# A fused attention and gated-FFN kernel on one core: another order of all five queues, another choice of engines, and one transposition done another way

## The chip, the core and the metric

The kernel runs on one core of one Trainium2 chip. The core has five instruction queues that run side by side and meet only through semaphores: TensorE (PE in the profile; its weight loads are shown apart as PEld), VectorE (DVE), ScalarE (ACT), GpSimd (POOL) and SyncE (SP). POOL and SP mostly issue DMAs here. The metric is the device time of one execution in microseconds. Three runs of the kernel before took 198.94 to 199.34 us, median 199.04.

## What is computed

Attention over pooled keys and values, then a feed-forward layer with a gated convolution over the sequence:

```python
k_p = k.reshape(B, H, Sp, 8, D).mean(axis=3)          # B=8, H=8, S=576, D=64, Sp=72
v_p = v.reshape(B, H, Sp, 8, D).mean(axis=3)
scores = np.matmul(q, k_p.transpose(0, 1, 3, 2)) / 8
attn = softmax(scores)
x = (attn @ v_p) as [B, S, 512]
h = np.maximum(x @ w_in, 0.0)                          # [B, S, 1024]
conv = sum over k in 0..2 of conv_w[k] * h shifted by k - 1 along S
out = (h * sigmoid(conv)) @ w_out                      # [B, S, 512], float32
```

Inputs are float32; the kernel computes in bfloat16 with float32 accumulation.

## The kernel before, in words

The batch elements b = 0..7 each go through the same stages; several are in flight at once.

- **Loads.** POOL issues DMAs that cast float32 to bfloat16: `ldk{b}.0` (512 rows of k, 512 KB as stored) and `ldk{b}.t` (64 rows), `ldv{b}.0` (512 KB; batch 0 has two of 256 KB, `ldv0.0` and `ldv0.1`) and four tails of 16 KB `ldv{b}.t0` to `.t3`, `ldq{b}` (576 KB), and the weights `ldwi0` (256 KB), `ldwi1`, `ldwo0`, `ldwo1`. POOL also builds the identity and, in five steps `mask0` to `mask4` (L371, L375), the mask that the v blocks need. k, v and q have two buffers each, so a load of batch b + 2 waits until batch b is done with its buffer.
- **Pooling.** DVE adds the eight rows of each pool (`kp1`, `kp2`, `ksum` for k, L414, L418, L443; `vp1`, `vp2`, `va`, `vb` for v). PE turns k (`kT`, L459), ACT or DVE copies it out (`kz`, L465).
- **q.** It has to be turned, too, and there are three ways: straight from the loaded layout in pairs of heads (`qTP`, L545, three groups of 16 matmuls with 64 columns of weights), from a regrouped copy (`qg` on DVE, L257, then `qT`, three groups of 8 matmuls with 128 columns), or by a transposing DMA from the regrouped copy (`qD` on SP, L566). `PARAMS["alt"]` says which batch uses which.
- **Attention.** `sc` (scores, five tiles per batch), `exp` on ACT (L610), `av` (attention times v with the row sums, L628 and L632, five tiles), `rc` and `nm` on DVE (reciprocal and normalising into `xx`, L641 and L645; four `xx` buffers), and the turn of x into `xT`: by matmul (`xt`, L659, and a copy `xte`) for batches 0 to 2, by a transposing DMA on SP (`xD`, L668) for 3 to 7.
- **Feed-forward.** `mm1.b.f` (eight matmuls of 288 columns, L700, for each of 8 blocks f of 128 hidden columns; it needs all five tiles of `xT`), `relu` on ACT (L706), then the convolution. In most blocks it is three steps outside PE: two scalings `cp0` and `cp2` (ACT L722 or DVE L724), two additions `ca0` and `ca2` (DVE L729, L734); in ten blocks PE does it (L753). `tanh` on ACT (L741, L758), `tg1` and `g` on DVE (L785, L791) make the gated product gT for two blocks at once.
- **Output.** `mm2.pair.t.c` (eight matmuls of 512 columns, L813, one tile of 128 rows; two batch elements form a pair with nine tiles), `oe` copies the tile out (ACT L836), `st` on SP stores one or two tiles (L840). For the last pair the tiles 4 to 8 are done in two pieces, so that only two of the eight products wait for the last gate.
- **Fillers.** Before some PE steps stand products of a zero tile (`fill`, L227), which compute nothing and keep PE occupied. The kernel has 238 of them.

No order follows from loops at run time. `Planner.add` numbers each step in the order in which the program text makes it, and `PARAMS["order"]` is a list of these numbers; each engine gets its steps in the order in which they stand in that list. `123@A1` also says which PSUM buffer the step takes (three of two banks, A0 to A2, and two of one bank, B0 and B1), and `23A1/93@B0` puts 23 fillers ahead of step 93. `PARAMS["act"]` names the steps that run on ACT where DVE could do them as well. The durations in the `add` calls have no effect on what runs.

```python
if slot:
    self.held[o.take] = (slot[0], int(slot[1]))
e = next(iter(o.eng)) if len(o.eng) == 1 else "ACT" if o.name in self.on_act else "DVE"
out.append((e, o, warm))
```

Of the kernel before, what the change touches and what calls it, by code (L numbers as in the profile page):

```python
# [13 lines left out]

PARAMS = {
    "order": (
# [40 lines left out]
    ),  # L57
    "act": (
# [8 lines left out]
    ),  # L67
    "alt": {"w": 1, "q1": 1, "c0.5": 2, "c0.7": 2, "q2": 1, "c1.1": 1, "c1.3": 2, "q3": 1, "x3.0": 1, "x3.1": 1, "x3.2": 1, "x3.3": 1, "x3.4": 1, "c2.1": 1, "c2.5": 1, "q4": 1, "x4.0": 1, "x4.1": 1, "x4.2": 1, "x4.3": 1, "x4.4": 1, "c3.5": 1, "q5": 1, "x5.0": 1, "x5.1": 1, "x5.2": 1, "x5.3": 1, "x5.4": 1, "q6": 2, "x6.0": 1, "x6.1": 1, "x6.2": 1, "x6.3": 1, "x6.4": 1, "q7": 2, "x7.0": 1, "x7.1": 1, "x7.2": 1, "x7.3": 1, "x7.4": 1},
    "nq": 2,
    "nr": 1,  # L70
    "nx": 4,
# [849 lines left out]
```

## Time and profile before

| what | before |
|---|---|
| median of 3 runs | 199.04 us (198.94 to 199.34) |
| the profiled execution's own time | 199.99 us |
| its span, first to last instruction | 198.3 us |
| granted clock of TensorE | 1.000 |
| DMA packets | 30.41 MB, mean 153 GB/s |
| POOL's queue (loads) | 16.00 MB |
| SP's queue (stores, transposes) | 14.11 MB |

How to read the profile: the page gives busy time by engine, the span in 40 slices, the chain of work that ended last (each piece follows from what released it), and groups of instructions with busy time, mean duration, and the idle time just before them with what ended it. The timeline lists instructions in order of time, with a bracket where the engine was idle before; the windows give each engine's busy time in a stretch.

### The profile page before, as it was taken

The page shows a single profiled execution, that of the slowest core. Times are in us where ns is not written, and L with a number is a line of the kernel's source. Part 1 is how long each engine was busy: PE and PEld are TensorE (multiplying, and loading weights), DVE is VectorE, ACT ScalarE, POOL GpSimd, SP SyncE. Part 2 cuts the span into 40 slices and gives each one's busy share as a digit, 9 for nine tenths or more (in the row PEclk, how much of TensorE's full clock was granted, in tenths as well). Part 3 has the DMA queues.
Part 4 walks back from the last instruction along what each step waited for, and adds up shares of the span by engine and source line. Part 5 has one row for each costly group of instructions (what it writes and reads, how often), then busy time and mean ns, then how long its engine had stood idle before and what let it go on. Part 6 is the DMA issues. An engine that isn't in the chain of part 4 may idle for free.

```text
span 198.3 us, 4826 instructions
## 1 busy us (share of the span) xinstructions
PE 190.1 (96%) x1890; PEld 132.3 (67%) x1905; DVE 164.1 (83%) x375; ACT 172.0 (87%) x314; POOL 48.3 (24%) x87
## 2 busy tenths in 40 slices
PE   7899989999999999999999999999999999999992
PEld 7897866776677878856866665766666655555441
DVE  3246759999949999999899999999999999899620
ACT  0559999992679999999999999999999899999931
POOL 7878425347225630080006100000000000000000
PEclk9999999999999999999999999999999999999999
DMA  6999999999999999999987999691401844043244
GB/s 134 169 135 150 188 205 205 206 191 142 204 196 185 152 192 60 197 113 197 172 232 158 194 213 166 120 164 26 172 3 27 266 144 161 1 148 117 106 164 159
DMA packets 40763, 30.41 MB, mean 153 GB/s; under 512 B 18572, under 2 KB 36004, under 8 KB 40740
## 3 DMA queue, kind: packets, MB, share of 16 engines
q0 software_dynamic: 18272, 16.00, 56.5%
q1 hardware_dynamic: 22468, 14.11, 31.4%
q8 instruction: 15, 0.25, 0.5%
q14 instruction: 8, 0.07, 0.1%
HBM read 32.52 MB, written 9.44 MB: 212 GB/s over the span
## 4 chain that ended last, share of the span: by engine, by line
PE 48%; ACT 16%; DMA 14%; DVE 12%; POOL 4%; issue 4%; ACTq 0%; DVEq 0%; POOLq 0%
PE psfA L700 16%; PE psfB L813 14%; DMA k_b<-in_k_dram 10%; ACT tg L741 5%; DMA v_b<-in_v_dram 4%; PE psfA L628 4%; ACT cv L722 3%; ACT hT L706 3%; PE psfA L753 2%; PE psfA L602 2%; ACT osb L836 2%; DVE cv L724 2%; POOL v_b L282 2%; DVE gT L791 2%; PE psfA L632 2%
## 5 line engine op out<-in xcount | busy, mean ns | idle before, releaser
L813 PE MATMUL psfB<-w_out,gT 128*128 128x512 bf16 (+1 forms) x259 | 62.6, 377 | 1.0 <-issue 0.2
L700 PE MATMUL psfA<-xT,w_in 128*128 128x288 bf16 x448 | 61.9, 286 | 0.1
L700 PEld LDWEIGHTS <-w_in 128*128 128x128 bf16 x448 | 43.0, 98 | 13.1 <-issue 0.8
L813 PEld LDWEIGHTS <-gT 128*128 128x128 bf16 x290 | 27.7, 98 | 28.8 <-DVE gT L791 1.0
L741 ACT ACTIVATE tg<-cv,cs 128x576 bf16<-128x576 bf16 x54 | 41.2, 789 | 0.3
L706 ACT ACTIVATE hT<-psfA 128x576 bf16<-128x576 f32 x56 | 36.6, 665 | 1.4 <-PE psfA L700 0.9
L645 DVE TENSOR_TENSOR xx<-psfA,rr 128x512 bf16<-128x512 f32 x40 | 27.1, 686 | 0.7
L722 ACT ACTIVATE cv<-hT,cr 128x576 bf16<-128x576 bf16 x35 | 26.9, 783 | 0.1
L724 DVE TENSOR_SCALAR cv<-hT,cr 128x576 bf16<-128x576 bf16 x73 | 25.9, 377 | 0.9 <-ACT hT L706 0.7
L282 POOL DMA_DIRECT2D v_b<-in_v_dram x32 | 16.8, 531 | 33.9 <-DVE vs L491 31.1
L836 ACT COPY osb<-psfB 128x512 f32<-128x512 f32 x33 | 19.2, 591 | 5.9 <-PE psfB L813 5.5
L791 DVE TENSOR_TENSOR gT<-tg,hT 128x1152 bf16<-128x1152 bf16 x32 | 23.9, 751 | 0.3
L610 ACT ACTIVATE attnT<-psfA 128x576 bf16<-128x576 f32 x35 | 22.7, 675 | 0.3
L734 DVE TENSOR_TENSOR cv<-cv 128x1152 bf16<-128x1152 bf16 (+1 forms) x29 | 20.7, 713 | 1.0 <-ACT cv L722 0.3
L729 DVE TENSOR_TENSOR cv<-cv,hT 128x1152 bf16<-128x1152 bf16 (+1 forms) x29 | 20.6, 711 | 0.3 <-ACT cv L722 0.2
L227 PEld LDWEIGHTS <-zero 128*128 128x128 bf16 x238 | 15.6, 105 | 1.7 <-DVE zero L318 1.1
L628 PE MATMUL psfA<-vblk,attnT 128*128 128x130 bf16 x160 | 15.9, 221 | 0.4 <-DVE xx L645 0.3
L785 DVE TENSOR_SCALAR tg<-tg 128x1152 bf16<-128x1152 bf16 x32 | 14.2, 448 | 2.2 <-ACT tg L741 2.0
L628 PEld LDWEIGHTS <-attnT 128*128 128x128 bf16 x160 | 11.8, 98 | 4.4 <-DVE xx L645 0.6
L227 PE MATMUL pswA<-zero 128*128 128x128 bf16 x192 | 13.3, 235 | 1.1 <-DVE zero L318 1.1
L414 DVE TENSOR_TENSOR k_b<-k_b 128x1280 bf16<-128x1280 bf16 x8 | 6.7, 840 | 6.8 <-DMA k_b<-in_k_dram 6.8
L641 DVE RECIPROCAL rr<-psfA 128x8 f32<-128x8 f32 x40 | 7.7, 198 | 5.2 <-PE psfA L632 5.1
(95 smaller groups left out, 234.1 us busy)
## 6 DMA issues: line engine op xcount, KB each, us to landing
out_dram<-osb SPq DMA_DIRECT2D x14, 512.0 KB, 3.2
k_b<-in_k_dram POOLq DMA_DIRECT2D x8, 512.0 KB, 8.5
q_b<-in_q_dram POOLq DMA_DIRECT2D x7, 576.0 KB, 8.2
v_b<-in_v_dram POOLq DMA_DIRECT2D x7, 512.0 KB, 12.2
out_dram<-osb SPq DMA_DIRECT2D x7, 256.0 KB, 2.1
w_out<-in_moe_w_out_dram POOLq DMA_DIRECT2D x2, 512.0 KB, 11.8
wf<-in_moe_w_in_dram SPq DMA_DIRECT2D x1, 512.0 KB, 5.3
k_b<-in_k_dram POOLq DMA_DIRECT2D x8, 64.0 KB, 6.3
```

The source lines that it names most:

```text
L227: nc.tensor.matmul(out=t, lhsT=zero[:, 0:P], rhs=zero[:, 0:P], start=True, stop=True)
L610: nc.scalar.activation(out=at(m)[:, t, :].rearrange("p (r i j) -> p r i j", i=2, j=3), in_=slot(key)[:, :, 0:HC].rearrange("p i (j r) -> p ...
L628: nc.tensor.matmul(out=a[:, g, c * w:(c + 2) * w], lhsT=attnT[m][:, S * s + u0:S * s + u0 + P], rhs=vblk[m][:, 2 * s:2 * s + 2, :].rearran ...
L645: nc.vector.tensor_tensor(out=xx[i3].rearrange("p (g h e) -> p g h e", g=2, h=4), in0=av_view()[:, :, :, 0:D], in1=rr[i3].rearrange("p (g ...
L700: nc.tensor.matmul(out=t[:, i, 0:HC], lhsT=w_in[:, c, f * P:(f + 1) * P], rhs=xT[m][:, c, i * HC:(i + 1) * HC], start=(c == 0), stop=(c == ...
L706: nc.scalar.activation(out=hT[m][:, f, 2:S + 2].rearrange("p (i x) -> p i x", i=2), in_=slot(key)[:, :, 0:HC], func=ACT.Relu)
L722: nc.scalar.activation(out=cv[y][:, kk // 2, z, :], in_=src, func=ACT.Copy, scale=sc)
L724: nc.vector.tensor_scalar(out=cv[y][:, kk // 2, z, :], in0=src, scalar1=sc, scalar2=None, op0=OP.mult)
L741: nc.scalar.activation(out=tg[i3][:, z, :], in_=cv[y][:, 0, z, :], func=ACT.Tanh if half else ACT.Sigmoid, scale=cs[:, f + z:f + z + 1] if ...
L791: nc.vector.tensor_tensor(out=o_, in0=tg[i3], in1=hT[b % 2][:, f:f + 2, 2:S + 2], op=OP.mult)
L813: nc.tensor.matmul(out=a[:, 0, j0:j1], lhsT=g[:, c, t * P:(t + 1) * P], rhs=w_out[:, c, j0:j1], start=(c == 0), stop=(c == n_fb - 1), skip ...
L836: copy_on(e)(out=osb[i3][:, x, :], in_=slot(key)[:, 0, :])
```

## The change

The program text and the load sizes stay. Three entries of `PARAMS` change: the order (whole), the set of steps on ACT (whole), and one choice of how q is turned.

```diff
     "order": (
-        "59 0 45 58 2 40 49 46 39 50 41 57 56 48 13 1 16 3 57A0/4@B0 17 5 43 18 6 12A0/83@B0 36 53 7 20 52 84 55 61 69 38 23 54 28 14 73 25 "
...
+        "2 0 40 58 59 41 50 46 44 49 45 39 54 57 56 53 43 1 55 3 62A0/4@B0 70 5 27 26 18A0/83@B0 61 52 30 24 20 28 84 51 13 32 25 73 62 74 "
...
     "act": (
-        "dw1.0 dw7.0 qTe.0.1.0 wc2.1 dw7.2 dw2.2 dw4.1 dw3.1 dw5.0 qTe.0.0.0 qTe.0.0.1 kz.0.1 dw4.2 dw4.0 dw6.0 dw5.1 dw5.2 wc2.0 xte.0.0 "
...
+        "dw4.0 dw3.2 wc2.1 dw5.0 dw3.0 dw1.2 dw4.1 qTe.0.1.0 dw5.2 dw3.1 kz.0.0 kz.0.1 qTe.0.0.1 dw2.1 dw6.0 wc2.0 xte.0.0 dw1.1 dw2.2 "
...
-    "alt": {"w": 1, "q1": 1, ... "q3": 1, "x3.0": 1, ...},
+    "alt": {"w": 1, "q1": 1, ... "x3.0": 1, ...},
```

The last line sends q of batch 3 from the turn in pairs to the turn from a regrouped copy: two DVE copies are added (`qg.3.0`, `qg.3.4`), 48 matmuls become 24. The kernel has 1073 steps after and 1071 before. The numbers stand for names; with the names put in, the queues read as follows.

POOL, from the start to the loads of batch 2:

```
before: ldq0.1 ldk0.0 ldk0.t ldq0.0 ldv0.t3 zh1 mask0 ident mask3 mask4 zh0 ldv0.t0 ldv0.1 ldv0.t2
        ldv1.t2 ldv0.t1 mask1 ldv0.0 mask2 ldq1 ldk1.t ldwi0 ldk1.0 ldwi1 ldk2.t ldv1.t0 ldv1.t3 ldk2.0 ldq2
after:  ldq0.1 ldk0.t ldk0.0 ldv0.t1 ldq0.0 ldv0.t3 ldv0.t0 zh0 ident ldv0.t2 ldv1.t3 ldv0.1 ldv0.0
        mask0 ldwi0 mask1 mask3 ldq1 mask4 mask2 ldk1.t ldk1.0 zh1 ldv1.t2 ldwi1 ldk2.t ldk2.0 ldq2
```

POOL around the loads of batch 3, and from where batch 6's v may be loaded:

```
before: ldk3.t ldv3.t3 ldk4.t ldv3.t1 ldk3.0 ldq3 ldk4.0 ldv3.0 ldv3.t0 ldv3.t2 ldv4.t3 ldk5.t ldk5.0 ldq4
after:  ldk3.t ldk3.0 ldv3.t0 ldq3 ldk4.0 ldv3.t2 ldk4.t ldv3.t1 ldv3.t3 ldv4.t1 ldv3.0 ldk5.t ldk5.0 ldq4 ldq5
before: ldv6.t3 ldv5.t3 ldv6.t1 ldv6.t0 ldk7.t ldv6.t2 ldv6.0
after:  ldv6.t2 ldv6.t1 ldv6.t0 ldv6.t3 ldv6.0
```

SP in the middle of the kernel:

```
before: st.0.0 xD.4.1 qD.6.1 xD.4.0 qD.6.0 xD.4.2 st.0.4 st.0.5 xD.4.3 xD.4.4 st.0.2 st.0.7 xD.5.0
        xD.6.0 st.1.0 xD.6.2 xD.6.1 xD.6.3 xD.6.4 st.1.2 st.1.4
after:  st.0.0 xD.4.0 qD.6.0 qD.6.1 st.0.2 xD.4.3 st.0.4 xD.4.4 xD.4.2 xD.4.1 xD.5.1 xD.5.0 st.0.5 st.0.7
        xD.6.0 xD.6.1 xD.6.3 st.1.5 st.1.4 xD.6.2 xD.6.4 st.1.2
```

PE around the first `mm1` of batch 4, and at the end:

```
before: sc.5.4 mm2.0.7.0 sc.6.1 mm1.3.7 sc.6.2 mm2.0.8.0 mm1.3.6 mm1.4.1 sc.6.0 mm1.4.3 av.5.0
after:  mm1.3.6 sc.6.1 mm1.3.7 sc.6.2 sc.5.4 mm2.0.7.0 mm1.4.3 sc.6.0 mm1.4.1 av.5.0 mm2.0.8.0
before: ... mm1.7.0 mm2.3.1.0 mm1.7.7 mm2.3.2.0 mm1.7.6 mm2.3.3.0 mm2.3.4.0 mm2.3.5.0 mm2.3.6.0 mm2.3.4.6 ...
after:  ... mm1.7.1 mm2.2.6.0 mm1.7.6 mm2.2.7.0 mm2.2.8.0 mm2.3.0.0 mm2.3.1.0 mm2.3.2.0 mm2.3.3.0 mm2.3.4.0 mm2.3.5.0 mm2.3.6.0 mm2.3.4.6 ...
```

Fillers: 238 before, 204 after. Of these 150 and 154 stand before the last turn of batch 0 (k or q), and 88 and 50 between that and the first `mm2`. On ACT, the scalings of the convolution go from 35 to 38; in the copies that follow a turn (`qTe`, `xte`) ACT has four fewer and DVE four more. Of the steps that may run on either engine, 63 change sides.

More of the change, by code (lines that the diff above doesn't have):

```diff
@@ L16 @@
     "order": (
[40 rows of a table removed]
[40 rows of a table added]
     ),
     "act": (
[8 rows of a table removed]
[8 rows of a table added]
     ),
-    "alt": {"w": 1, "q1": 1, "c0.5": 2, "c0.7": 2, "q2": 1, "c1.1": 1, "c1.3": 2, "q3": 1, "x3.0": 1, "x3.1": 1, "x3.2": 1, "x3.3": 1, "x3.4": 1, "c2.1": 1, "c2.5": 1, "q4": 1, "x4.0": 1, "x4.1": 1, "x4.2": 1, "x4.3": 1, "x4.4": 1, "c3.5": 1, "q5": 1, "x5.0": 1, "x5.1": 1, "x5.2": 1, "x5.3": 1, "x5.4": 1, "q6": 2, "x6.0": 1, "x6.1": 1, "x6.2": 1, "x6.3": 1, "x6.4": 1, "q7": 2, "x7.0": 1, "x7.1": 1, "x7.2": 1, "x7.3": 1, "x7.4": 1},
+    "alt": {"w": 1, "q1": 1, "c0.5": 2, "c0.7": 2, "q2": 1, "c1.1": 1, "c1.3": 2, "x3.0": 1, "x3.1": 1, "x3.2": 1, "x3.3": 1, "x3.4": 1, "c2.1": 1, "c2.5": 1, "q4": 1, "x4.0": 1, "x4.1": 1, "x4.2": 1, "x4.3": 1, "x4.4": 1, "c3.5": 1, "q5": 1, "x5.0": 1, "x5.1": 1, "x5.2": 1, "x5.3": 1, "x5.4": 1, "q6": 2, "x6.0": 1, "x6.1": 1, "x6.2": 1, "x6.3": 1, "x6.4": 1, "q7": 2, "x7.0": 1, "x7.1": 1, "x7.2": 1, "x7.3": 1, "x7.4": 1},
     "nq": 2,
```

92 rows, old and new, of the table PARAMS are left out of this document.

## The prediction

> **What bounds the kernel now.** I read the page first: the busy table, the clock line and the costliest groups.
>
> ```profile
> span 198.3 us, 4826 instructions
> PE 190.1 (96%) x1890; PEld 132.3 (67%) x1905; DVE 164.1 (83%) x375; ACT 172.0 (87%) x314; POOL 48.3 (24%) x87
> PEclk9999999999999999999999999999999999999999
> L813 PE MATMUL psfB<-w_out,gT 128*128 128x512 bf16 (+1 forms) x259 | 62.6, 377 | 1.0 <-issue 0.2
> L700 PE MATMUL psfA<-xT,w_in 128*128 128x288 bf16 x448 | 61.9, 286 | 0.1
> ```
>
> Three engines are nearly full, and the clock is never cut. Since matmuls overlap, a busy PE says little; spacing does. Next come two stretches by engine, and pieces of the chain that ended last.
>
> ```profile
> 20.00:45.00 25.00, 24.14 (x331) 18.55 (x329) 21.03 (x49) 23.87 (x54) 10.15 (x17) 1.00 1.22 198
> 45.00:194.30 149.30, 147.83 (x1243) 97.54 (x1256) 134.80 (x297) 136.98 (x233) 21.99 (x35) 1.00 0.83 146
> 16.03 11.00 DMA k_b<-in_k_dram
> 27.12 0.84 DVE k_b L414
> 48.20 1.73 PE psfB L813 x8
> 137.11 3.92 PE psfA L700 x32
> ```
>
> The columns are PE, PEld, DVE, ACT, POOL, then clock, DMA share and GB/s. One group of eight L813 matmuls takes 1.73 us and one L700 matmul 3.92/32 = 0.1225 us. From 45 us on, PE is idle for 149.30 - 147.83 = 1.5 us only. L700 (448 of them) and 36 groups of L813 alone are 54.9 + 62.3 = 117 of these 149 us; scores, attn·v, turns and convolutions come between. So from 45 us on the end is: when the first L813 group starts, plus PE's work, plus what PE loses. Only three things can pay: an earlier start of that stage, fewer losses in it, or a shorter tail.
>
> The start of that stage hangs on DVE. Batch 1's k load is issued at 16.03 and lands at 27.03; DVE starts on it at 27.12 and runs without a break to the last gate product of batch 0:
>
> ```profile
> 43.45 1.42 DVE L791 TENSOR_TENSOR gT<-tg,hT 128x1152 bf16<-128x1152 bf16 x2
> 45.17 1.89 PE L813 MATMUL psfB<-w_out,gT 128*128 128x512 bf16 x7
> ```
>
> The product ends at 44.87 and the first L813 group follows.
>
> **The change part by part.** *1, the early loads (POOL).* In the windows of 1 us the last two columns are DMA share and GB/s; then POOL's own order in time.
>
> ```profile
> 12.00:13.00 1.00, 1.00 (x20) 0.92 (x17) 0.96 (x5) 0.00 (x0) 1.00 (x2) 1.00 0.83 121
> 13.00:14.00 1.00, 0.76 (x36) 0.63 (x36) 0.71 (x2) 0.00 (x0) 0.99 (x3) 1.00 0.39 37
> 14.00:15.00 1.00, 1.00 (x37) 0.96 (x31) 0.19 (x1) 0.95 (x2) 1.00 (x3) 1.00 0.88 118
> 15.00:16.00 1.00, 1.00 (x19) 0.89 (x16) 1.00 (x5) 0.95 (x3) 1.00 (x2) 1.00 1.03 159
> 16.00:17.00 1.00, 0.97 (x11) 0.53 (x10) 0.57 (x3) 0.98 (x3) 1.00 (x3) 1.00 0.59 45
> 2.08 8.71 DMA k_b<-in_k_dram
> 11.07 0.49 POOL L282 DMA_DIRECT2D v_b<-in_v_dram  x1 [1.67 <-DMA k_b<-in_k_dram]
> 11.56 0.98 POOL L375 TENSOR_SCALAR_AFFINE_SELECT mask<-mask 128x260 bf16<-128x260 bf16 x1
> 12.50 0.75 POOL L277 DMA_DIRECT2D v_b<-in_v_dram  x1
> 13.98 0.80 POOL L251 DMA_DIRECT2D q_b<-in_q_dram  x1
> 27.32 0.79 POOL L277 DMA_DIRECT2D v_b<-in_v_dram  x1 [3.91 <-DMA k_b<-in_k_dram]
> ```
>
> These five windows moved 480 KB where 198 GB/s (the row above) would have moved 990: 510 KB, 2.6 us, were lost because POOL issued late. The rows also show a rule: the load at 11.07 waits for the one issued eight loads earlier (2.08 + 8.71 = 10.79), and the load at 27.32 for the one eight earlier (16.03 + 11.00). A load can go only when the eighth before it has landed.
>
> In the new order the second 256 KB of v is the eleventh load, so it waits for the third, batch 0's k, and goes at about 11.3 instead of 12.50. The 256 KB of w_in follow after one memset, 1.5 us later, at about 12.9. Both fall into the hole. But POOL now sits before 11.3 with the masks still ahead of it, and q of batch 1 goes only after two more selects (0.98 and about half of that), near 15.1 instead of 13.98, and k near 17.6 instead of 16.03. The bytes ahead of k are the same in both orders. Bounds: half the hole closed, -1.3 us; POOL's extra wait passed on to k, +0.7 us. I take -0.3: early bytes gained are mostly lost again at q. Of DVE's list from there to the last product eight small operations leave (one copy of a turned q among them) and seven come (two such copies): 0.
>
> *2, q of batch 3 turned after regrouping on DVE instead of in pairs.* DVE gains two copies and PE has 24 matmuls instead of 48.
>
> ```profile
> L257 DVE COPY q<-q_b 96x1536 bf16<-96x1536 bf16 x4 | 2.2, 538 | 0.0
> 58.25 0.21 DVE L641 RECIPROCAL rr<-psfA 128x8 f32<-128x8 f32 x1 [2.57 <-PE psfA L632]
> 56.61 0.80 PE psbB L545 x32
> 64.89 0.45 PE psbB L659 x8
> ```
>
> The copies are 1.08 us and fit into the idle 2.57 us at that place; without that cover they cost their 1.08. PE spends 48 x 0.025 = 1.2 us on the pairs now; 24 single ones cost between half of it and, at the 0.45/8 = 0.056 us of the 128-column transposes of L659, 1.3. I take 0, bounds -0.6 to +0.2.
>
> *3, SP's queue for batch 4.* Before, the first L700 of batch 4 starts when its last transposed tile lands.
>
> ```profile
> 91.54 1.20 SPq L668 DMA_TRANSPOSE xT<-xx  x1
> 92.84 2.18 SPq L566 DMA_TRANSPOSE qT<-q  x1
> 95.12 1.62 SPq L668 DMA_TRANSPOSE xT<-xx  x1
> 96.79 1.37 SPq L566 DMA_TRANSPOSE qT<-q  x1
> 98.27 2.15 SPq L668 DMA_TRANSPOSE xT<-xx  x1
> 100.50 1.01 SPq L840 DMA_DIRECT2D out_dram<-osb  x2
> 101.61 2.89 SPq L668 DMA_TRANSPOSE xT<-xx  x2
> 105.53 2.12 PE L700 MATMUL psfA<-xT,w_in 128*128 128x288 bf16 x16
> DMA to landing us min/median/max: 3.1/3.8/5.8
> DMA to landing us min/median/max: 2.3/2.4/3.1
> ```
>
> SP never pauses from 91.54 to 104.50: five x transposes, two q transposes, two stores. The last is issued at about 103.3 and lands 3.1 later at 106.4; the second half of the 105.53 row, batch 4's first group, starts at 106.4, with no slack. The new order gives SP the same nine, starting with tile 0, whose normalising comes second (0.7 to 0.8 us later), while PE loses one L813 group (1.73) ahead of that point. So PE comes 1.7 us earlier to tiles that come 0.8 later: +2.5 at worst. The two landing rows are the x transposes of 84 to 112 us, with loads in flight, and of 140 to 165, with none. The new POOL order sends batch 6's v four issues of half a microsecond after its buffer is free instead of six, so it clears sooner; with x transposes near the 1.20 of the first row SP needs some 2 us less, and the cost falls to 0. Bounds 0 to +2.5; I take +0.6. Behind the waiting L700 stand scores, attn·v and the last L813 tile of the pair, hence ACT.
>
> [...]
>
> *4, the tail.* The last L700 group now has eleven L813 tiles behind it instead of six.
>
> ```profile
> 185.34 1.19 PEld L813 LDWEIGHTS <-gT 128*128 128x128 bf16 x7 [0.42 <-DVE gT L791]
> 189.65 4.65 PEld L813 LDWEIGHTS <-gT 128*128 128x128 bf16 x24 [0.54 <-DVE gT L791]
> ```
>
> PE waits 0.42 + 0.54 = 0.96 us for gates of batch 7. With five more tiles (8.6 us) between, they should be ready. ACT has the same work before its last tanh, so not all is sure: -0.8, bounds -0.96 to 0. Engine choices only trade (35 scalings on ACT become 38, turns go the other way): 0.
>
> **Sum.** -0.3 + 0 + 0.6 - 0.8 = -0.5 us. The profiled execution took 199.99 (span 198.3 and 1.7 around it), so it would take 199.5; the median of the runs, 199.04, is 0.95 lower, and becomes 198.5.
>
> **The rivals.** *SP starves PE.* Part 3 at its worst, +2.5, and the same again for batch 6, where a store of two tiles, which waits for their L813 groups, now stands before the last two transposes (+0.5, half of the 1.01 us row of two stores): -0.3 + 3.0 - 0.8 = +1.9, 200.9; with batch 4 alone 200.4. It decides from the point where the nine issues take over 11.5 us. For it: zero slack now; against: the lighter loads. *The loads gain fully.* Part 1 at -1.3 and part 3 at 0: -2.1, 196.9. For it: 510 KB missing; against: the masks behind the eight-load wait. *No change that can be told* (0.2%, 0.4 us, is what a measurement here can tell from none): the load gain is nil, transposes cost 1.0, the tail gives 0.8: 199.2; this is also the case that the reordering does nothing where PE is bound. *The clock is cut.* Fillers between the first scores and the first L813 fall from 88 to 50. Were PE granted half for one slice of the page (4.96 us), 2.5 us are lost: 201.0. The clock row shows full speed through all gaps, the 0.76-busy window at 13 us too.
>
> [...]
>
> **How the numbers follow.** Forecast 0.41 (198.5, its own range 197.8 to 199.0), full gain 0.15, no change 0.12, SP starves 0.28, clock 0.04. Faster takes the full gain and three quarters of the forecast, 0.46; same the rest of the forecast and most of no change, 0.21; slower 0.33. The range 196.6 to 200.7 holds the unknown costs of parts 1 and 3 and leaves out the two ends.
>
> **What would show it.** Part 1: the first DVE k_b row of batch 1 near 26.8 and the first L813 near 44.9. Part 2: no idle DVE beyond a microsecond before the 58 us reciprocal. Part 3: PE idle before batch 4's first L700 near 104 us, released by a transpose. Part 4: no DVE gT wait in the last 15 us. Wrong would be a first L813 off by over a microsecond, or a PE loss over 1.5 us at another place.

## The result: 204.7 us, 2.9% slower, and the profile after

| | before | changed |
|---|---|---|
| median of 4 runs each, same chip | 199.19 us (198.94 to 199.61) | 204.68 us (204.12 to 206.16) |
| ratio | | 1.0285, 95% interval 1.0226 to 1.0344 |
| the profiled execution: time, span | 199.99, 198.3 us | 204.99, 202.9 us |
| granted clock of TensorE | 1.000 | 0.992 (0.983 to 0.992 in the four runs) |

The page of the changed kernel, the lines that answer to those of before:

```profile
span 202.9 us, 4715 instructions
PE 190.0 (94%) x1833; PEld 131.8 (65%) x1847; DVE 165.8 (82%) x378; ACT 170.9 (84%) x313; POOL 47.6 (23%) x87
PEclk9999999999999999999699999999999999999999
...
L700 PE MATMUL psfA<-xT,w_in 128*128 128x288 bf16 x448 | 62.1, 291 | 0.0
```

Busy times are almost those of before, so nothing became dearer by its work. What is new stands in the clock line: slice 20 of 40, near 97 to 101 us, ran at six tenths. The view of waits between 88 and 132 us (who waited for whom: sum, count, longest) shows what stands ahead of it:

```profile
ACT osb L836 <- DMA out_dram<-osb: 4.2, 1, 4.2
...
PE psbB L459 <- ACT osb L836: 3.1, 1, 3.1
...
PE psfA L602 <- DMA qT<-q: 1.3, 1, 1.3
```

PE stood 3.1 us behind a copy of an output tile on ACT, and that copy stood 4.2 us behind a store. The chain of waits of the changed kernel through that place, then its timeline there (all engines), then two rows of PE's own:

```profile
86.26 8.62 DMA out_dram<-osb
...
95.49 0.67 ACT cv L722
96.16 0.55 ACT hT L706
```

```profile
85.71 0.84 POOL L277 DMA_DIRECT2D v_b<-in_v_dram  x1
86.26 0.58 SPq L840 DMA_DIRECT2D out_dram<-osb  x1
...
94.90 0.59 ACT L836 COPY osb<-psfB 128x512 f32<-128x512 f32 x1 [4.20 <-DMA out_dram<-osb]
95.54 0.44 PE L459 MATMUL psbB<-ident,ksum 128*128 128x128 bf16 x5 [3.10 <-ACT osb L836]
```

```profile
96.75 0.40 PE L628 MATMUL psfA<-vblk,attnT 128*128 128x130 bf16 x4 [0.78 <-ACT hT L706]
...
97.30 3.67 PE L700 MATMUL psfA<-xT,w_in 128*128 128x288 bf16 x16
```

The reader can follow it by names. `st.0.0` stores the first two output tiles from the output buffer `osb` 0; it is issued at 86.26 and lands 8.62 us later. There are three such buffers, so `oe.0.5`, the copy of the sixth tile, needs buffer 0 again and waits for that landing. In ACT's list a scaling and a relu stand behind `oe.0.5` (94.90); they start at 95.49 and 96.16, one after the other. PE's `kT.6` (L459) needs the PSUM buffer that `oe.0.5` empties, and the next `av` the one that the relu empties. Then 16 L700 matmuls take 3.67 us where 16 x 0.1225 = 1.96 are their time at full clock.

In the kernel before, the same store was issued just ahead of the same 512 KB of v (`ldv6.0`, L277) instead of just behind them. Its timeline (all engines):

```profile
88.56 0.59 SPq L840 DMA_DIRECT2D out_dram<-osb  x1
88.71 0.78 POOL L277 DMA_DIRECT2D v_b<-in_v_dram  x1
...
93.07 0.59 ACT L836 COPY osb<-psfB 128x512 f32<-128x512 f32 x1 [0.29 <-DMA out_dram<-osb]
```

How long the load took stands in the chain of the kernel before, then in the changed kernel's DMA view (its last figure is us from issue to landing):

```profile
88.71 8.13 DMA v_b<-in_v_dram
```

```profile
v_b<-in_v_dram POOLq DMA_DIRECT2D x1, 512.0 KB, 9.0
```

Before: store 88.56, load `ldv6.0` 88.71; the store is down at 93.05, well ahead of the load (88.71 + 8.13 = 96.84). Changed: load 85.71, store 86.26; the store lands at 94.88, with the load (94.7). A step of 0.7 us in the relative order of two queues made the store 4.1 us longer.

To see where time went over the whole kernel, take PE's delay at a step: its start (that of its first weight load), less the time of all PE work ahead of it (1.73 us for a group of eight L813, 0.98 for eight L700, 0.74 for a convolution, 0.34 for an `av`, 0.24 for a `sc`, and so on; 169.05 us in both kernels, fillers not counted). Where the delay grows, PE lost time. The last three columns are kernels of the experiments below.

| PE's delay (us) at | before | changed | change | early store | and two stores later | and q of batch 7 |
|---|---|---|---|---|---|---|
| the first L813 group | 21.85 | 20.57 | -1.28 | 20.70 | 20.43 | 20.84 |
| `sc.5.1` (85 to 87 us) | 23.13 | 21.36 | -1.77 | 21.48 | 21.22 | 21.63 |
| `mm1.3.1` (95 to 101 us) | 23.60 | 27.57 | +3.97 | 21.83 | 21.58 | 21.98 |
| `mm1.4.1` (104 to 110 us) | 23.66 | 27.77 | +4.11 | 22.93 | 21.78 | 22.18 |
| `mm1.5.7` (131 to 141 us) | 24.47 | 29.31 | +4.84 | 23.94 | 22.81 | 23.01 |
| first L813 of the last pair | 24.72 | 29.72 | +5.00 | 24.34 | 23.20 | 23.38 |
| the last L813 group | 25.26 | 29.90 | +4.64 | 24.52 | 23.39 | 23.56 |

The changed kernel reaches 85 us ahead by 1.77, then loses 6.2 us at the one place (21.36 to 27.57, of which before lost 0.47), 0.7 more near 131 us, and gains 0.4 in the tail. The end is 4.64 us later, as the spans say (4.6). The times of the two profiled executions differ by 5.0: another 0.4 us lie outside the span (204.99 - 202.9 against 199.99 - 198.3), and 2.0 to 2.2 us (in two executions 2.3 and 2.7) instead of 1.7 to 1.8 lie there in the kernels made from the changed one; where they come from was not tried.

### The profile page after: what moved, and what is told of

It reads as the page before. It is cut to its first block, busy times and chain, and to the rows that moved or that the text cites. A ratio compares the mean times of both kernels' runs of the same rounds, so it can differ in the third digit from the quotient of the medians.

```text
span 202.9 us, 4715 instructions
## 1 busy us (share of the span) xinstructions
PE 190.0 (94%) x1833; PEld 131.8 (65%) x1847; DVE 165.8 (82%) x378; ACT 170.9 (84%) x313; POOL 47.6 (23%) x87
## 3 DMA queue, kind: packets, MB, share of 16 engines
q1 hardware_dynamic: 22468, 14.11, 26.8%
## 4 chain that ended last, share of the span: by engine, by line
PE 58%; ACT 21%; DMA 15%; POOL 2%; issue 2%; SPq 0%; ACTq 0%; POOLq 0%
PE psfB L813 25%; PE psfA L700 22%; DMA out_dram<-osb 4%; DMA q_b<-in_q_dram 4%; ACT attnT L610 4%; DMA k_b<-in_k_dram 4%; ACT hT L706 3%; PE psfA L628 3%; ACT tg L741 3%; ACT qT L552 2%; ACT hT L691 2%; DMA qT<-q 2%; ACT tg L758 2%; PE psfA L813 2%; PE psfA L602 2%
## 5 line engine op out<-in xcount | busy, mean ns | idle before, releaser
L813 PE MATMUL psfB<-w_out,gT 128*128 128x512 bf16 (+1 forms) x261 | 61.6, 377 | 0.8 <-issue 0.2
L700 PE MATMUL psfA<-xT,w_in 128*128 128x288 bf16 x448 | 62.1, 291 | 0.0
L700 PEld LDWEIGHTS <-w_in 128*128 128x128 bf16 x448 | 44.1, 99 | 14.6 <-issue 0.7
L813 PEld LDWEIGHTS <-gT 128*128 128x128 bf16 x290 | 27.8, 98 | 29.5 <-issue 0.9
L836 ACT COPY osb<-psfB 128x512 f32<-128x512 f32 x33 | 20.1, 610 | 12.4 <-PE psfB L813 8.2
L722 ACT ACTIVATE cv<-hT,cr 128x576 bf16<-128x576 bf16 x38 | 29.3, 794 | 0.1
L282 POOL DMA_DIRECT2D v_b<-in_v_dram x32 | 16.1, 506 | 46.5 <-DVE cv L724 20.6
L724 DVE TENSOR_SCALAR cv<-hT,cr 128x576 bf16<-128x576 bf16 x70 | 24.3, 368 | 2.3 <-ACT hT L706 1.3
L227 PEld LDWEIGHTS <-zero 128*128 128x128 bf16 x204 | 13.8, 107 | 1.6 <-DVE zero L318 1.1
L227 PE MATMUL pswA<-zero 128*128 128x128 bf16 x171 | 12.2, 239 | 1.1 <-DVE zero L318 1.1
L602 PE MATMUL psfA<-qT,kz 128*128 128x288 bf16 x56 | 11.2, 286 | 1.4 <-DMA qT<-q 1.3
```

Of the source, the lines that this page charges most:

```text
L227: nc.tensor.matmul(out=t, lhsT=zero[:, 0:P], rhs=zero[:, 0:P], start=True, stop=True)
L700: nc.tensor.matmul(out=t[:, i, 0:HC], lhsT=w_in[:, c, f * P:(f + 1) * P], rhs=xT[m][:, c, i * HC:(i + 1) * HC], start=(c == 0), stop=(c == ...
L722: nc.scalar.activation(out=cv[y][:, kk // 2, z, :], in_=src, func=ACT.Copy, scale=sc)
L724: nc.vector.tensor_scalar(out=cv[y][:, kk // 2, z, :], in0=src, scalar1=sc, scalar2=None, op0=OP.mult)
L813: nc.tensor.matmul(out=a[:, 0, j0:j1], lhsT=g[:, c, t * P:(t + 1) * P], rhs=w_out[:, c, j0:j1], start=(c == 0), stop=(c == n_fb - 1), skip ...
```

## The experiments

**Theory T**: `ldv6.0` overtook `st.0.0`, so the store lands with the load; ACT, then PE, wait for it; the pause cuts the clock. **Rivals**: S, SP's order for batch 4 costs the time; F, the smaller number of fillers costs it; and, for the store, that it is slow there whatever the order.

**One more output buffer.** `oe.0.5` then has a buffer of its own.

```diff
-    "nos": 3,
+    "nos": 4,
```

> The changed kernel with a fourth output buffer, so that the copy oe.0.5 need not wait until the store st.0.0 has left its buffer; order, engines and load sizes stay. Theory T (the store st.0.0 lands late, the copy oe.0.5 waits 4.2 us for it on ACT, PE stands 3.1 us behind ACT, and then the clock is halved for 2 to 3 us): both losses go, 3.4 + 2.6 = 6.0 us, so about 198.7 us against 204.7, clock 1.000, no idle stretch of PE over 1 us between 90 and 100 us. Rival S (SP's order for batch 4, part 3 of the prediction, is what costs): nothing changes, 204 to 205. Rival F (the clock falls because the whole stretch holds fewer fillers): the stall goes but the clock does not come back, about 202.

Measured 200.36 us, ratio to before 1.0048 (1.0016 to 1.0081). 4.3 of the 5.5 us are gone, no slice lost clock near 97 us. The longest wait of PE between 84 and 132 us in this kernel:

```profile
PE psfA L700 <- DMA xT<-xx: 1.5, 1, 1.5
```

Nothing waits for a store. But 198.7 was expected, and 1.7 us are missing: with the pause gone, PE comes to the first L700 of batch 4 before its last transposed tile has landed. S is wrong as the cause of the 5.5 us and right as what comes next.

**The store ahead of batch 3's transposes.**

```diff
 SP: ... xD.3.0
+        st.0.0
         xD.3.3 xD.3.2 xD.3.1 xD.3.4
-        st.0.0
         xD.4.0 qD.6.0 qD.6.1 ...
```

> The changed kernel with only st.0.0 moved in SP's queue, from behind the four transposes of batch 3 to ahead of them (issue near 70 us instead of 86.3). Theory T: the copy oe.0.5 finds its buffer free, about 198.7 us, clock 1.000; what the four transposes lose behind a store of half a microsecond's issue is at most 0.5. Rival S: 204 to 205. If st.0.0 drags through loads there too but is done by 88, T still holds.

Measured 199.99 us, 1.0005 (0.9975 to 1.0034): one entry in one queue gives back the whole loss. The time is still 1.3 us above the expected 198.7. ACT runs through (`oe.0.5` without a bracket), but the wait for batch 4's x is there again, here 0.73 us (1.1 by PE's delay). ACT, then PE, of this kernel:

```profile
90.67 0.62 ACT L836 COPY osb<-psfB 128x512 f32<-128x512 f32 x1
...
104.04 1.15 PE L700 MATMUL psfA<-xT,w_in 128*128 128x288 bf16 x8 [0.73 <-DMA xT<-xx]
```

**The mirror in the kernel before: `ldv6.0` first.**

```diff
 POOL: ...
+        ldv6.0
         ldv6.t3 ldv5.t3 ldv6.t1 ldv6.t0 ldk7.t ldv6.t2
-        ldv6.0
         ldv7.t0 ...
```

> The kernel before with only POOL's queue changed: ldv6.0 (512 KB) ahead of the six small loads behind which it stands, so that it goes near 85.1 us instead of 88.7 and so ahead of st.0.0 (88.56) instead of behind it. Theory T: st.0.0 lands several microseconds later than 93.05, the copy oe.0.5 waits as in the changed kernel; a wait of PE of 2 us or more and, from about 3 us on, a cut clock: 201 to 205 us. Rival (the overtaking is not what makes the store late): within 0.4 of 199.2.

Measured 205.41 us, 1.0281 (1.0234 to 1.0327), 0.4 us above the expected range: the loss appears in the kernel before. But its profile shows two causes at once, so this run alone decides nothing. The waits of this kernel between 84 and 104 us:

```profile
DVE v_b L414 <- DMA v_b<-in_v_dram: 4.6, 1, 4.6
...
PE psfA L700 <- DVE xx L645: 3.6, 1, 3.6
...
ACT osb L836 <- DMA out_dram<-osb: 2.1, 1, 2.1
```

The 16 KB of `ldv5.t3`, now behind the 512 KB in the same queue, landed about 1 us after them (93.82 and 92.9), and DVE waited 4.6 us for them. So the next run leaves `ldv5.t3` in front:

```diff
 POOL: ... ldv6.t3 ldv5.t3
+        ldv6.0
         ldv6.t1 ldv6.t0 ldk7.t ldv6.t2
-        ldv6.0
```

> The kernel before with ldv6.0 moved ahead of four small loads only, and behind ldv5.t3, which the earlier run had held up together with the store: ldv6.0 goes near 86.1 us instead of 88.7, so some 2 us ahead of st.0.0. Theory T: st.0.0 lands near 95 us instead of 93.05, the copy oe.0.5 on ACT waits some 2 us for it, PE loses about 1 to 2 us there and, short of 3 us of idling, keeps its clock: 200.5 to 202. Rival (the earlier run's loss was ldv5.t3 alone): 199.2 to 199.7, as before.

Measured 201.83 us, 1.0119 (1.0071 to 1.0166), within the expected range, though the waits are longer than expected. The timeline of this kernel (all engines), a piece of its chain, and two windows:

```profile
85.64 0.83 POOL L277 DMA_DIRECT2D v_b<-in_v_dram  x1
...
87.82 1.08 SPq L840 DMA_DIRECT2D out_dram<-osb  x1
...
94.59 1.03 PE L700 MATMUL psfA<-xT,w_in 128*128 128x288 bf16 x7 [2.85 <-DMA xT<-xx]
...
96.39 0.59 ACT L836 COPY osb<-psfB 128x512 f32<-128x512 f32 x1 [4.08 <-DMA out_dram<-osb]
```

```profile
86.54 8.01 DMA xT<-xx
```

```profile
92.00:95.50 3.50, 0.91 (x8) 0.74 (x9) 1.18 (x2) 0.31 (x1) 0.00 (x0) 1.00 1.58 211
95.50:99.00 3.50, 3.50 (x21) 2.35 (x19) 2.67 (x7) 2.34 (x4) 0.00 (x0) 0.51 0.97 192
```

The load goes at 85.64; the store, issued 2.2 us behind it, takes 8.55 us and holds `oe.0.5` for 4.08; a transpose issued 0.9 us behind it takes 8.01 and holds PE for 2.85. The clock was expected to hold short of 3 us of idling, an estimate: the two cuts seen until then stood behind waits of 3.10 and 3.59 us. In this profiled execution it did not: the last columns of the windows are clock, DMA share and GB/s, and the clock is 0.51 for 3.5 us. But this execution, 203.48 us, is the longest of the five; the other four took 201.36 to 202.64 us with a granted clock of 0.996 to 1.000, so in the median the loss is the waits alone.

**The store only one place earlier**, 0.7 us ahead of the load:

```diff
 SP: ... xD.3.3 xD.3.2 xD.3.1
-        xD.3.4 st.0.0
+        st.0.0 xD.3.4
```

> The changed kernel with st.0.0 one place earlier only, ahead of the transpose xD.3.4 instead of behind it: it is issued near 85.0 us, 0.7 ahead of ldv6.0 (85.7) instead of 0.55 behind. Theory T (what SP issues just ahead of a 512 KB load is done in 4 to 5 us, what it issues just behind lands with the load): st.0.0 lands near 89.5, no wait of oe.0.5, 199.5 to 200.4 us. But xD.3.4 then goes near 85.6 and is the one that can be dragged: then PE waits up to 3 us for it at the first L700 of batch 3, 202 to 204. Rival (the store is slow near this load whatever the order): lands near 94, 204 to 205.

Measured 201.00 us, 1.0086 (1.0056 to 1.0116), between the two cases foretold. The store, issued at 84.65, takes 3.45 us. The transpose `xD.3.4` is now issued within 0.05 us of the load and takes 5.64, where it took 2.6 to 3.1 in the kernels that issue it 0.7 us ahead of the load; PE waits for that one. The timeline of this kernel and a piece of its chain:

```profile
84.65 0.58 SPq L840 DMA_DIRECT2D out_dram<-osb  x1
...
85.38 0.84 POOL L277 DMA_DIRECT2D v_b<-in_v_dram  x1
...
90.25 0.62 ACT L836 COPY osb<-psfB 128x512 f32<-128x512 f32 x1
...
91.02 1.03 PE L700 MATMUL psfA<-xT,w_in 128*128 128x288 bf16 x7 [0.85 <-DMA xT<-xx]
```

```profile
85.33 5.64 DMA xT<-xx
```

So in these runs it is the order against the load that decides, not the place as such (the store took 3.45 us issued 0.73 ahead of the load, 8.62 issued 0.55 behind it): what SP issued in the profiled kernels from 0.1 to 2.8 us behind the 512 KB load, a store or a transpose, landed with it or up to 2.3 us after it. In the changed kernel the store is down at 94.88, 0.2 us behind the load (94.70). The load took longer as well: 9.0 us with the store behind it, and 5.9 in the DMA view of the kernel with the early store:

```profile
v_b<-in_v_dram POOLq DMA_DIRECT2D x1, 512.0 KB, 5.9
```

By what means the two hold each other up, and whether bandwidth alone would make the store late, no run here shows.

**Is the clock a loss of its own?** Fillers in PE's pause, in a PSUM buffer that comes free 1.0 us into it:

```diff
-771@B1        (kT.6)
+36A2/771@B1   (36 fillers ahead of it, and kT.6 after nm.4.2 in the list)
```

> The changed kernel with 36 fillers ahead of kT.6, which run from the moment nm.4.2 has emptied its PSUM buffer (about 93.4 us): PE's wait for the copy stays, but PE is not idle in it for more than about 1.2 us. Theory T: the clock stays at 1.000, the 2.6 us go, the 3.4 stay: about 202.1 us. If the clock has no part in it: 204.7. If fillers hold kT.6 back, up to 0.5 more than that.

Measured 204.41 us, 1.0199 (1.0121 to 1.0277; the ratio leaves out the longest of the four runs): not the 202.1 expected. With 8 instead of 36:

> The changed kernel with 8 fillers (0.5 us) instead of 36 in PE's wait for the copy: idle of about 1.0 us, 0.5 us of fillers, idle of about 1.6 us. If the clock falls for one unbroken idle stretch of some 3 us, it stays at 1.000 here, and the time is that of 36 fillers less what chance does: 203 to 204.4 us. If it falls for the share of idle time over some microseconds, the slice near 97 us shows about 0.6 again: 204.7.

Measured 204.29 us, 1.0245 (1.0209 to 1.0280). Windows of the changed kernel, of the one with 36, and of the one with 8 fillers; the columns are length, PE, PEld, DVE, ACT, POOL, clock, DMA share, GB/s:

```profile
92.00:96.00 4.00, 0.88 (x12) 0.64 (x11) 1.26 (x3) 1.10 (x2) 0.00 (x0) 1.00 1.08 184
...
97.00:100.50 3.50, 3.50 (x19) 2.21 (x17) 2.60 (x5) 2.49 (x5) 0.00 (x0) 0.51 0.70 208
```

```profile
94.00:98.00 4.00, 2.62 (x41) 2.39 (x42) 0.62 (x1) 1.77 (x4) 0.00 (x0) 1.00 1.08 143
```

```profile
92.00:96.00 4.00, 1.27 (x17) 0.85 (x15) 1.03 (x3) 1.57 (x3) 0.00 (x0) 1.00 1.11 169
96.00:99.50 3.50, 3.22 (x17) 2.27 (x17) 2.33 (x5) 2.54 (x5) 0.00 (x0) 0.51 0.83 231
```

```profile
93.24 0.62 PE L227 MATMUL pswA<-zero 128*128 128x128 bf16 x8 [1.03 <-DVE xx L645]
95.07 0.44 PE L459 MATMUL psbB<-ident,ksum 128*128 128x128 bf16 x5 [1.21 <-ACT osb L836]
96.28 0.59 PE L628 MATMUL psfA<-vblk,attnT 128*128 128x130 bf16 x4 [0.78 <-ACT hT L706]
```

The last three rows are PE with 8 fillers: no idle stretch is over 1.21 us, and the clock is halved all the same. So one unbroken pause was not needed here. What sets the three kernels apart in these rows is how much PE did in the microseconds before: it was busy 0.88 and 1.27 of 4 us where a cut followed, 2.62 of 4 where none did. Four of the fourteen profiled executions have a cut. In the changed kernel it goes from 97.09 to 100.50, 3.41 us at a clock of 0.50; in as long a stretch right ahead of the cut PE was busy 0.62, 0.77, 0.93 and 1.06 us in the four. The emptiest 3.41 us that no cut followed, between 10 and 190 us of all fourteen, held 1.81. It lies in the kernel with all edits of SP's queue, further below (columns as above):

```profile
118.60:122.01 3.41, 1.81 (x19) 0.84 (x18) 3.41 (x11) 2.37 (x5) 0.00 (x0) 1.00 1.13 310
```

No run tried whether there is a limit of busy time; if there is, these executions leave it between a share of 0.31 (1.06 of 3.41) and one of 0.53 (1.81 of 3.41). F in the form "fewer fillers elsewhere" falls: nothing changed elsewhere.

3.41 us at 0.50 cost at most 1.7 us, not the 2.6 that T gave the cut. The mirror kernel with `ldv5.t3` in front agrees: 203.48 us with the cut, 201.36 to 202.64 without; and the changed kernel's longest run, 206.16 us, has twice the loss of clock (0.983) of the other three (204.12 to 204.99 us, 0.990 to 0.992). The delays say the same: from `sc.5.1` to `mm1.3.1` PE loses 6.2 us without fillers and 4.8 with 36 (22.58 to 27.34). That 1.4 does not show in the end for two reasons: the execution with 36 fillers came to its first L813 1.2 us late (44.84 against 43.61), by the scatter of the early loads, and 0.9 us were lost again at batch 4's first L700, which the longer stall had hidden. Four runs that spread from 202.25 to 205.37 (the last at a granted clock of 0.994) can't tell 1.4 us.

**The next wait: SP's order for batch 4.** Two stores go behind its transposes, besides the early `st.0.0`:

```diff
 SP: ... xD.4.0 qD.6.0 qD.6.1
-        st.0.2 xD.4.3 st.0.4 xD.4.4 xD.4.2 xD.4.1
+        xD.4.3 xD.4.4 xD.4.2 xD.4.1 st.0.2 st.0.4
```

> The changed kernel with the early st.0.0 and, besides, SP's stores st.0.2 and st.0.4 moved from among the transposes of batch 4 to behind them. Theory X (with the stall gone, PE waits about 1.1 us for the last x transpose of batch 4, and the two stores ahead of it are what makes it late; part 3 of the prediction): the last transpose goes about 0.9 us earlier and PE's loss at the first L700 of batch 4 falls from 1.1 to about 0.2: 0.9 under the kernel with the early store alone (199.99), so 199.1. Rival (the transposes wait for the normalising on DVE, not for SP): no gain, 200.0.

Measured 199.28 us, 0.9989 (0.9961 to 1.0018). By the medians that is 0.7 of the expected 0.9, by the ratios 0.3, and the intervals overlap; the time alone doesn't tell. In the profile no wait of PE stands ahead of that L700 any more, and in PE's delay the loss there falls from 1.1 to 0.2. X holds as to the cause.

**The wait near 125 to 131 us: q of batch 7.** First the two halves change places, then they stand side by side.

```diff
 SP: ... st.0.5 st.0.7
-        qD.7.0 xD.5.3 qD.7.1 xD.5.2
+        qD.7.1 xD.5.3 qD.7.0 xD.5.2
```

> The same, and the two transposes of q of batch 7 change places in SP's queue, so that qD.7.1, for which the scores sc.7.3 wait, goes first. Theory Q (the 1.2 us that PE loses near 125 us are the wait for qD.7.1, landed at 125.6 where it would land at 123.2): another 0.9 to 1.2 us, about 198.0 us, faster than the kernel before (199.2 to 199.7) by 1.2 to 1.7. Rival (the scores then wait for the other half or another tile): 199.1.

Measured 199.52 us, 1.0010 (0.9984 to 1.0037): no gain. PE starts the scores at 125.58, when the other half has landed (125.48). In the code `sc` reads all six tiles of q, which I had overlooked: PE waits for whichever half comes second. The view of waits puts PE's 1.6 us there down to a scaling on ACT, which the scores don't read; so this rests on the landing and the code.

```diff
-        qD.7.0 xD.5.3 qD.7.1 xD.5.2
+        qD.7.0 qD.7.1 xD.5.3 xD.5.2
```

> The changed kernel with the early st.0.0, the two stores behind batch 4's transposes, and qD.7.1 moved directly behind qD.7.0 (ahead of one x transpose), since the scores sc.7.3 need both halves of q and so wait for whichever comes second. Theory Q2: the second half lands near 122.7 instead of 124.4, ahead of the time (123.3) at which PE comes to the scores; PE's loss there (0.8 in the kernel with the two edits of the stores) goes: 199.28 - 0.8 = 198.5 us, 0.7 under the kernel before. Rival (two q transposes side by side only slow each other, or the x tile pushed back is then waited for): 199.3.

Measured 199.01 us, 0.9992 (0.9967 to 1.0017), 0.5 us above the expected 198.5. The second half lands at 123.64, later than foretold, and PE starts the scores at 123.65. The wait for q is gone from the profile; what stays is 0.3 us for the x tile pushed back, which the last edit was to remove:

```diff
-        xD.5.2 st.1.0 xD.5.4
+        xD.5.2 xD.5.4 st.1.0
```

> The kernel with all edits of SP's queue so far (early st.0.0, two stores behind batch 4's transposes, the two halves of batch 7's q side by side) and st.1.0 behind the last x transpose of batch 5 instead of ahead of it. That transpose goes 0.6 us earlier, which is all of the 0.3 us that PE still waits for it at the first L700 of batch 5: 199.0 - 0.3 = 198.7 us, 0.6 under the kernel before if its runs stand at 199.3. Rival (the store, now later, holds up a copy on ACT, or 0.3 us is lost in the scatter of the early loads): 199.0 as before the edit.

Measured 199.21 us, 0.9993 (0.9964 to 1.0023): no gain that can be told. Its 12 runs go from 197.91 to 200.68, and the profiled one shows where such a spread can come from: the tile view of k between 100 and 125 us, with its issue, the wait and the landing.

```profile
L265 POOL DMA_DIRECT2D k_b<-in_k_dram x1: 776/776/776, 104.7 to 104.7; - x1
...
  DMA k_b<-in_k_dram: 2.0, 1
...
DMA to landing us min/median/max: 10.3/10.7/11.1
```

Batch 7's k was issued at 104.7 as in the kernel before this edit (104.8), but took 11.1 us instead of 7.9. The new DVE order asks for it near 114.3 and has the normalising of x behind it, so 1.5 us of the 2.0 reached PE.

**The early loads alone**: the kernel before with POOL's first 31 entries in the new order.

> The kernel before with POOL's queue in the changed kernel's order up to and with the second batch's v (31 entries, the steps of the mask among them), all else as before. Theory E (part 1 of the change brings the first L813 forward by 1.2 us through the earlier k of batch 1): k_b of batch 1 starts on DVE near 25.0 instead of 27.1, the first L813 near 43.7 to 44.3 instead of 44.9, the end 0.6 to 1.2 us earlier: 198.0 to 198.6. Rival (the gain needs DVE's new order too): within 0.3 of the kernel before.

Measured 198.85 us, 0.9983 (0.9957 to 1.0010), too close to tell by time. In its profile the k_b row of batch 1 starts at 24.82 and the first L813 comes at 44.35 instead of 44.89: but the mirror kernel with the old early order came to it at 44.42 once. So k comes earlier by POOL's order alone; how much of the earlier stage that brings is left open. No version here is faster than the kernel before by more than its interval.

## Why the prediction was wrong, by its own steps

The step that broke the forecast is in part 3: it counted the earlier load `ldv6.0` as relief and put at nothing what it does to the store `st.0.0`. The runs showed a stall there that cost PE 6.2 us, cut clock included. The parts one by one:

**Part 1, the early loads** (-0.3, bounds -1.3 to +0.7): right in kind, too small. DVE and PE of the changed kernel:

```profile
25.03 0.82 DVE L414 TENSOR_TENSOR k_b<-k_b 128x1280 bf16<-128x1280 bf16 x1 [0.54 <-DMA k_b<-in_k_dram]
...
43.67 1.89 PE L813 MATMUL psfB<-w_out,gT 128*128 128x512 bf16 x7
```

k starts 2.1 us earlier and the stage 1.3 (first weight load, 44.89 to 43.61); foretold were rows at 26.8 and 44.9, so the L813 row, at 43.67, came 1.2 us ahead of its forecast. That was a named sign of a wrong forecast, too. Over all profiled executions the first L813 comes at 43.29 to 44.84 with the whole new early order (ten, mean 43.8) and at 44.42 to 45.24 with the old one (three, mean 44.9): 1.1 us, near the lower bound. What failed in this part was that the early bytes are "mostly lost again at q". q went at the old time, 13.97, since the two selects ahead of it took 0.83 us together where I had put 0.98 and about half of that, and the 256 KB of weights between v and q were down at 18.3 us instead of 22.5. The wait of a load for the eighth before it held: the second part of v went at 11.10, 0.29 us behind the landing of batch 0's k (10.81), and in the traces of both kernels none of the 62 loads from the ninth on goes less than 0.28 us behind the landing of the eighth before it. Batch 1's k itself was issued 0.5 us later than before (16.57), but took 8.4 us instead of 11.0. POOL, and two windows:

```profile
13.21 0.83 POOL L375 TENSOR_SCALAR_AFFINE_SELECT mask<-mask 128x260 bf16<-128x260 bf16 x2
13.97 0.79 POOL L251 DMA_DIRECT2D q_b<-in_q_dram  x1
```

```profile
12.00:13.00 1.00, 1.00 (x22) 1.00 (x20) 0.97 (x3) 0.13 (x1) 1.00 (x2) 1.00 1.19 190
13.00:14.00 1.00, 1.00 (x51) 0.90 (x50) 0.93 (x3) 0.59 (x2) 0.99 (x4) 1.00 1.17 177
```

121 and 37 GB/s became 190 and 177: the hole was filled.

**Part 2, q of batch 3** (0): right. DVE took the copies in without being late, and no wait of DVE over 0.2 us is left between 50 and 62 us, where it had stood for 2.57:

```profile
53.37 1.02 DVE L257 COPY q<-q_b 96x1536 bf16<-96x1536 bf16 x2
```

**Part 3, SP and batch 4** (+0.6, bounds 0 to +2.5): the wait exists and is larger, 1.1 us in the kernel with the early store and 1.8 in the one with four output buffers by PE's delay; but it shows only once the stall is gone. In the changed kernel PE comes so late that the tiles have landed, so the sign I had given for it (idle ahead of the first L700 of batch 4) is absent there. The step that broke the forecast stands here: the new POOL order, it says, "sends batch 6's v four issues of half a microsecond after its buffer is free instead of six, so it clears sooner". The load did go earlier. I booked it as relief for the transposes behind it and did not ask what it would now stand in front of. The store `st.0.0` was on the table as one of SP's entries, ahead of the stretch that I costed, with 4.5 us to its landing and a copy that had already waited 0.29 us for it and began 0.02 us after it: a step without slack, which I had not listed.

**Part 4, the tail** (-0.8, bounds -0.96 to 0): half of it. The waits for gates are gone; one row holds 40 matmuls without a break:

```profile
182.79 9.01 PE L813 MATMUL psfB<-w_out,gT 128*128 128x512 bf16 x40
```

PE's delay over the last pair grows by 0.18 where it grew by 0.54, so 0.4 us.

**Not in the sum at all:** the stall, 6.2 us with the cut clock (about 4.5 and 1.7, an estimate from the 3.41 us at 0.50); the wait of the scores of batch 7, 1.3 us by the wait's row; and 0.4 us outside the span, which the sum took over from before as 1.7. Parts 1, 3 and 4 as measured would have made -1.1 + 1.1 - 0.4 = -0.4, near the forecast's -0.5, but by luck: they were off by 0.8, 0.5 and 0.4, and the errors cancel; "a PE loss over 1.5 us at another place" was the named sign of a wrong forecast, and that is what came. The rival with the cut clock had the right symptom and about the right price for it (2.5 us against 1.7), but from the number of fillers, and at 201.0 it left out the pause itself. Its half for one slice was an assumption; the runs showed 0.50 for 3.41 us, and in the kernel with 8 fillers the cut came behind idle stretches of 1.03, 1.21 and 0.78 us.

## What to carry to other kernels

When a large load is moved earlier in one queue, list every transfer of the other queues that it now overtakes, and ask who waits for each and with what slack: the store `st.0.0`, whose buffer was needed again at once, stood on the critical path with 8.62 us, though it only writes results. Its stall was paid by the steps behind it in the lists, too (4.2 us on ACT; 6.2 of PE's delay, cut clock included), so the slack of the first waiter (0.02 us before) said little about the price; and in the four executions where PE was busy for a share of no more than 0.31 of 3.41 us, the clock took up to 1.7 us more (at 0.53 it held). When a large stall is removed, expect the next wait (here 1.1 to 1.8 us) to have been hiding under it, and cost a repair with that in the sum.

## What the runs showed of the hardware that was not expected

- A 512 KB store issued 0.6 or 2.2 us behind a 512 KB load of another queue took 8.1 to 8.7 us (6.9 at 2.8 us behind), transposes issued 0.1 to 1.5 us behind it 7.3 to 8.2; issued 0.15 to 0.8 us ahead, the store took 3.4 to 4.5 us. Two transposes that went in the last half microsecond ahead of the load took 5.6 and 5.7 us.
- TensorE's clock was halved for 3.4 us in four profiled executions, after 3.41 us in which PE was busy 0.62 to 1.06 us, in one case with no idle stretch over 1.21 us; no cut followed 1.81 of 3.41 us. In the mirror kernel with `ldv5.t3` in front one execution of five had the cut (mean clock 0.991; the other four 0.996 to 1.000).
- The same load, issued at the same time in two kernels whose queues are the same up to there, landed 3.2 us apart (batch 7's k: 7.9 and 11.1 us).
